# Chunk steps at explicit places, sums in place of clamps, and weight narrowing shared with ScalarE: one change to a fused gated-recurrence and feed-forward kernel

## The chip, the cores and the metric

The kernel runs on one NeuronCore of a Trainium2 chip. The metric is device time in microseconds (us) of one execution. A core has five engines with a queue each: TensorE (PE: matmuls, transposes; its weight loads are listed as PEld), VectorE (DVE), ScalarE (ACT), GpSimd (POOL) and SyncE (SP, which here only issues transfers). The kernel is written in a framework that tracks which instruction needs which tile, gives each tile a place in a pool, and schedules: it fixes the order of each engine's instructions when the program is built. The order in the source is the priority; an instruction whose inputs are ready by the framework's own timing may be put ahead of an earlier one. At run time each engine takes its instructions strictly in the fixed order.

## The reference

Two blocks. The first is a recurrence with complex gates, for 4 batches x 8 heads x 768 steps, head size 48:

```python
mag = np.sqrt(a_re * a_re + a_im * a_im)
scale = np.minimum(mag, 0.999) / (mag + 1e-06)
a_re_n, a_im_n = a_re * scale, a_im * scale
for t in range(S):
    S = a[t] * S + outer(k[t], v[t])        # complex a, per row of S
    y[t] = q[t] @ real(S)
```

The second takes y as 3,072 tokens x 384 and computes, with weights given as float64,

```python
h = x @ w_in                                   # 384 -> 2048
sp = np.maximum(h, 0.0) + np.log1p(np.exp(-np.abs(h)))
out = (h * erf(sp)) @ w_out                    # 2048 -> 384
```

## The kernel before

A unit is 256 tokens of one batch (two chunks of 128); there are 12. Everything of a unit is: its gates; the recurrence of its two chunks; its feed-forward in two slabs of 1,024 hidden columns; the output product.

*Gates.* `g_tan` squares a_re and a_im on ACT, adds on POOL, and makes the tangent: a clamp of a_re from below (L734), a reciprocal (L735), a product with a_im (L740), clamps of |a|^2 (L743) and of the tangent (L745). `g_turn` takes the arctangent on ACT; `g_angle` sums angles over the chunk with a matmul, brings the last row of the chunk before over by a small transfer (L761) and takes whole turns off; `g_sin` makes cosine and sine (tile CS, two buffers). `g_log` makes log magnitudes, `g_decay` sums them with a matmul (L805) and takes exponentials of both signs (tile pr, two buffers). A sum over `off` and `spans` at the end tells whether all values stayed in the range of this path; if not, a branch runs a slower second path (`product_path`).

*Chunk.* `chunk(u, c)` returns eleven steps: k and q times decay and turn (`prep`, L831 and L835), transposes into columns (`cols`, evacuated by ACT, L846), the scores with their mask (`scores`, L854 and L857), the state (`state`, L866 to L875), y (`y_`, evacuated by ACT, L890) and the transpose of y into x^T (`xT`, L899).

*Feed-forward.* `ff_in` makes h of a slab with 48 matmuls, evacuated by ACT (L916). `softplus` clamps h into z on DVE (L930), then runs Exp, Ln, Ln, Exp over 128 x 2,048 elements on ACT, into z and yy. `erf_times_h` works in four parts: t = z * yy on POOL (L948), then DVE and a Gelu on ACT that overwrites z, up to h times erf in place (L949, L951, L952). `ff_out` makes the output in 16 x 2 matmuls (L966), evacuated by ACT (L970). z and yy have one buffer each, h has four.

*Weights.* [...] `narrow` loads a piece as pairs of 32-bit words into a buffer of h and rebuilds float32 with integer operations: five passes on DVE and three more through `words` (a buffer of z), a product (L689) and a sum (L693) on POOL. There are six pieces of w_in (128 x 1,024) and eight of w_out (128 x 768).

*Order.* ACT holds tables for one set of functions at a time; every activation issued through `act` (L639) stands in one fixed chain in source order, with a table load (L638) at each change of set. Plain copies are outside of that chain. The source order comes from windows w = -2 to 13. Window w has the recurrence of unit w, the feed-forward of unit w-1, the output of unit w-2 and the gates of later units; `weave` spreads each list over a share of the window:

```python
wts = weights_in() if w == -1 else weights_out() if w == 0 else []
weave((0.0, 1.0, rec), (0.0, 0.05, only(w + 2, g_turn) + only(w + 1, g_sin)), (0.0, 0.9, wts),
      (0.0, 0.45, f0), (0.45, 0.9, f1), (0.2, 1.0, only(w - 2, ff_out)), ...)
```

Of the kernel before, what the change touches and what calls it, by code (L numbers as in the profile page):

```python
# [19 lines left out]
P = 128  # L20
# [9 lines left out]

SLOPE = 1.5

SPAN = 1e13
# [522 lines left out]
def quotient_path(  # L556
# [49 lines left out]
    dram = ctx.enter_context(tc.tile_pool(name="dram", bufs=4, space=bass.MemoryType.DRAM))  # L606
    ps_a = ctx.enter_context(tc.tile_pool(name="ps_a", bufs=2, space=PSUM))
# [17 lines left out]
    off = const.tile([P, NU], FP, name="off")  # L625
    spans = const.tile([P, NU * C], FP, name="spans")
# [36 lines left out]
    def load_qkv(u):  # L663
        if u < NU:
            load(ldq, "q", q, u)
            load(ldq, "k", k, u)
            load(ldq, "v", v, u, bufs=2)


    def narrow(dst, src, shape):  # L670
# [4 lines left out]
        raw = hp.tile([P, n], I64, tag="h", name="raw")  # L675
        tmps = zp.tile([P, 2, n], U32, tag="z", name="words")
# [5 lines left out]
        a, b = tmps[:, 0], tmps[:, 1]  # L682
        nc.vector.tensor_scalar(out=a, in0=hi, scalar1=0x7FF00000, scalar2=None, op0=OP.bitwise_and)
        nc.vector.tensor_scalar(out=b.bitcast(FP), in0=a, scalar1=float(897 << 20), scalar2=None, op0=OP.is_ge)
# [4 lines left out]
        nc.gpsimd.tensor_tensor(out=f, in0=f, in1=b.bitcast(FP), op=OP.mult)  # L689
        nc.vector.tensor_scalar(out=a, in0=u, scalar1=0xFF800000, scalar2=None, op0=OP.bitwise_and)  # L690
        nc.vector.scalar_tensor_tensor(out=b.bitcast(FP), in0=lo, scalar=2.0**-52, in1=a.bitcast(FP),
                                       op0=OP.mult, op1=OP.mult)
        nc.gpsimd.tensor_tensor(out=f, in0=f, in1=b.bitcast(FP), op=OP.add)  # L693

    def weights_in():
# [3 lines left out]
        return [partial(narrow, w_in_sb[:, i, f0:f0 + n], w_in[i * P:(i + 1) * P, f0:f0 + n], (n,))  # L699
                for f0 in range(0, FF, n) for i in range(KD)]  # L700

    def weights_out():
        if w_out.dtype == FP:
            return [lambda: nc.gpsimd.dma_start(out=w_out_sb, in_=w_out.rearrange("(i p) e -> p i e", p=P))]
        return [partial(narrow, w_out_sb[:, i:i + 2, :].rearrange("p i e -> p (i e)"),
                        w_out[i * P:(i + 2) * P, :].rearrange("(i p) e -> p i e", p=P), (2, DM))
# [11 lines left out]
    def g_tan(u):  # L718
# [3 lines left out]
        def s0():  # L722
            s, y, m = t_("s"), t_("y"), t_("m")
            act(out=s, in_=ar, func=AF.Square)
# [4 lines left out]
            act(out=m, in_=m, func=AF.Relu, accum_out=off[:, u:u + 1])  # L729
            T["s"], T["y"] = s, y  # L730

        def s1():
            rec = t_("rec")
            nc.vector.tensor_scalar(out=rec, in0=ar, scalar1=2.0**-60, scalar2=None, op0=OP.max)  # L734
            nc.vector.reciprocal(out=rec, in_=rec)  # L735
            T["rec"] = rec

# [245 lines left out]
    for f in g_tan(0):  # L983
        f()
# [82 lines left out]
```

## Time and profile before

| what | value |
|---|---|
| time, median of 3 runs | 985.98 us (983.36 to 987.53) |
| the profiled execution's own time | 981.68 us |
| its span, first to last instruction | 980.0 us |
| PE, DVE, ACT, POOL busy | 812.8, 632.6, 579.6, 309.4 us |
| granted clock of PE, mean | 0.922 |
| x^T of a unit complete: units 0, 1, 2, 10, 11 | 128, 177, 313.5, 841.3, 901.3 us |

A row of a group reads: line, engine, operation, tiles out<-in, shapes, count, then busy time (us), mean duration of one (ns), and the idle time of the engine just before these instructions with what ended it. Matmuls overlap, so their mean is longer than their spacing. In the timeline a row starts with start and duration in us. The granted clock is the share of full speed that PE was given.

### The profile page before, as it was taken

How to read it: one execution, taken by the hardware profiler on the slowest of the kernel's cores; microseconds unless marked ns; L12 is line 12 of the kernel's file. 1: busy time of each engine (PE TensorE's matmuls, PEld its weight loads, DVE VectorE, ACT ScalarE, POOL GpSimd, SP SyncE). 2: the span in 40 equal slices, each digit the busy share in tenths (PEclk: the TensorE clock that was granted, in tenths of full speed). 3: DMA queues.
4: the chain of work that ended last, by engine and by line, in shares of the span. 5: the costliest groups of instructions: out<-in, count | busy, mean ns of one | idle time of the engine just before them, and what ended most of it. 6: DMA issues, size and time to landing. Idle time of an engine off the chain costs nothing. (4 is left out here: it accounts for less than half of the span.)

```text
span 980.0 us, 10235 instructions
## 1 busy us (share of the span) xinstructions
PE 812.8 (83%) x3882; PEld 618.2 (63%) x3882; DVE 632.6 (65%) x736; ACT 579.6 (59%) x737; POOL 309.4 (32%) x180
## 2 busy tenths in 40 slices
PE   0115788968849989999999898998999999999987
PEld 0004677755637767777767676776767786887654
DVE  6778987638687576865975965767647534664340
ACT  4515241236777777758568587677684766556650
POOL 3565443324342242431431423224302220132220
PEclk9998575888978989999999999999999899999989
DMA  7552333101030211120311211111011110000000
GB/s 171 133 151 71 86 81 97 49 0 33 2 77 19 34 33 33 33 49 18 65 33 23 43 33 34 33 33 33 7 27 34 33 33 1 17 1 17 1 16 20
DMA packets 148034, 41.77 MB, mean 43 GB/s; under 512 B 142068, under 2 KB 145160, under 8 KB 147208
## 3 DMA queue, kind: packets, MB, share of 16 engines
q1 hardware_dynamic: 147976, 41.03, 18.4%
q8 instruction: 32, 0.52, 0.2%
q14 instruction: 26, 0.21, 0.1%
HBM read 36.24 MB, written 4.75 MB: 42 GB/s over the span
## 5 line engine op out<-in xcount | busy, mean ns | idle before, releaser
L966 PE MATMUL ops<-w_out_sb,h 128*128 128x384 f32 x768 | 286.0, 512 | 16.6 <-DVE h L952 8.9
L914 PE MATMUL hps<-xT,w_in_sb 128*128 128x256 f32 x1152 | 267.8, 387 | 16.9 <-ACT h L916 14.6
L914 PEld LDWEIGHTS hps<-xT,w_in_sb 128*128 128x128 f32 x1152 | 220.3, 194 | 59.0 <-ACT h L916 15.9
L948 POOL TENSOR_TENSOR t<-z,yy 128x512 f32<-128x512 f32 x96 | 148.0, 1560 | 301.0 <-ACT yy L639 261.3
L639 ACT ACTIVATE z<-z 128x2048 f32<-128x2048 f32 (+1 forms) x144 | 152.2, 1057 | 119.9 <-POOL t L948 84.8
L966 PEld LDWEIGHTS ops<-w_out_sb,h 128*128 128x128 f32 x768 | 146.3, 200 | 99.7 <-issue 16.9
L949 DVE SCALAR_TENSOR_TENSOR yy<-t,yy 128x512 f32<-128x512 f32 x96 | 101.6, 1083 | 74.0 <-POOL t L948 74.0
L916 ACT COPY h<-hps 128x512 f32<-128x512 f32 x96 | 55.5, 581 | 86.1 <-PE hps L914 85.4
L951 DVE TENSOR_TENSOR z<-z,yy 128x512 f32<-128x512 f32 x96 | 88.0, 946 | 0.0
L882 PE MATMUL y<-v,A 128*128 128x48 f32 x384 | 77.2, 298 | 11.5 <-DVE A L857 11.5
L857 DVE TENSOR_TENSOR A<-sc,triu 128x512 f32<-128x512 f32 x48 | 32.7, 684 | 79.4 <-PE sc L854 79.4
L638 ACT ACT_TABLE_LOAD x64 | 82.1, 1283 | 1.1
L854 PEld LDWEIGHTS sc<-qT,kT 96*128 96x128 f32 x384 | 54.6, 214 | 44.5 <-ACT qT L846 40.3
L930 DVE TENSOR_SCALAR z<-h 128x1024 f32<-128x1024 f32 x48 | 42.2, 887 | 62.1 <-ACT h L916 59.9
L854 PE MATMUL sc<-qT,kT 96*128 96x128 f32 x384 | 61.0, 308 | 24.4 <-ACT qT L846 23.8
L765 PE MATMUL sum<-th,turns 128*128 128x384 f32 x48 | 26.4, 637 | 65.7 <-DVE th L762 50.6
L952 DVE SCALAR_TENSOR_TENSOR h<-z,h 128x512 f32<-128x512 f32 x96 | 78.4, 846 | 0.1
L882 PEld LDWEIGHTS y<-v,A 128*128 128x128 f32 x384 | 65.1, 216 | 16.1 <-DVE A L857 12.9
L885 PE MATMUL y<-S,qT 96*128 96x48 f32 x320 | 69.3, 302 | 0.0
L793 POOL TENSOR_TENSOR lr<-s,y 128x768 f32<-128x768 f32 x12 | 24.9, 2078 | 127.1 <-ACT y L639 97.0
L735 DVE RECIPROCAL rec<-rec 128x768 f32<-128x768 f32 x12 | 59.4, 4950 | 0.3
L885 PEld LDWEIGHTS y<-S,qT 96*128 96x128 f32 x320 | 56.0, 218 | 0.0
(80 smaller groups left out, 972.4 us busy)
## 6 DMA issues: line engine op xcount, KB each, us to landing
raw<-in_moe_w_in_dram SPq DMA_DIRECT2D x6, 1024.0 KB, 7.1
raw<-in_moe_w_out_dram SPq DMA_DIRECT2D x8, 768.0 KB
ar<-in_a_re_dram SPq DMA_DIRECT2D x24, 192.0 KB, 3.2
ai<-in_a_im_dram SPq DMA_DIRECT2D x24, 192.0 KB, 3.4
q<-in_q_dram SPq DMA_DIRECT2D x24, 192.0 KB, 3.6
k<-in_k_dram SPq DMA_DIRECT2D x24, 192.0 KB, 2.9
v<-in_v_dram SPq DMA_DIRECT2D x24, 192.0 KB, 3.8
out_dram<-o SPq DMA_DIRECT2D x24, 192.0 KB, 1.9
```

Source lines behind the costliest of these rows:

```text
L638: in_order(nc.scalar.preload_act_table_set(sets[0]))
L639: in_order(nc.scalar.activation(func=func, **kw))
L735: nc.vector.reciprocal(out=rec, in_=rec)
L854: nc.tensor.matmul(out=ps[:, j, :], lhsT=st["k", g][0:D2, j, :], rhs=st["q", g][0:D2, j, :], start=True, stop=True)
L882: nc.tensor.matmul(out=y[:, j, :], lhsT=st["A", g][:, i, :], rhs=T["v", u][:, c, j, :], start=True, stop=first)
L885: nc.tensor.matmul(out=y[:, j, :], lhsT=st["q", g][0:D2, i, :], rhs=T["S"][0:D2, j, :], start=False, stop=True)
L914: nc.tensor.matmul(out=ps[:, e, :], lhsT=w_in_sb[:, kd, f0:f0 + P], rhs=T["xT", u][:, kd, :], start=(kd == 0), stop=(kd == KD - 1))
L948: nc.gpsimd.tensor_tensor(out=t, in0=z, in1=y, op=OP.mult)
L949: nc.vector.scalar_tensor_tensor(out=y, in0=t, scalar=-2.0, in1=y, op0=OP.add, op1=OP.mult)
L951: nc.vector.tensor_tensor(out=z, in0=z, in1=y, op=OP.mult)
L952: nc.vector.scalar_tensor_tensor(out=h, in0=z, scalar=1.0 / RT2, in1=h, op0=OP.add, op1=OP.mult)
L966: nc.tensor.matmul(out=ps, lhsT=T["h", u, sl][:, e, jj * P:(jj + 1) * P], rhs=w_out_sb[:, i, :], start=(i == 0), stop=(i == KF - 1))
```

## The change

Six things change together.

1. `weave` gives way to explicit places. Each step of window w gets a number from 0 to 1 and the steps are issued in that order. A chunk's steps have places of their own, with the state and all transposes ahead of the scores. Weights are narrowed in windows -1 (two pieces), 0 (six) and 1 (six).
2. `narrow` has its own pool for the raw words (two buffers) and puts `words` into z and yy by turns. Two DVE passes and POOL's product go; Square and Exp on ACT with a sum take their place (they flag a zero weight), and the low words are scaled on ACT.
3. The clamps go: of h ahead of Exp, of a_re, |a|^2 and the tangent. Sums of squares, of exponentials and of reciprocals, taken by the activations that make these values (`accum_out`), are compared with limits at the end. The reciprocal of a_re becomes Ln and Exp on ACT.
4. In `erf_times_h` the product t moves from POOL to DVE, and Gelu writes a tile e (two buffers) in place of z.
5. The evacuations of q^T, of y and of the output move from ACT to DVE.
6. CS and pr have one buffer; the sums of `g_decay` become steps of their own; sine and arctangent come at the end of a window.

```diff
+    seen = [const.tile([P, n], FP, name=f"seen{i}") for i, n in enumerate((NU * C, NU, NU, NU * NSL, NU * NSL, 16))]
+    spans, off, large, exps, inverse, zeros = seen
     def narrow(dst, src, shape, i):
-        raw = hp.tile([P, n], I64, tag="h", name="raw")
-        tmps = zp.tile([P, 2, n], U32, tag="z", name="words")
+        raw = rawp.tile([P, n], I64, tag="raw", name="raw")
+        pool, tag = ((zp, "z"), (yp, "yy"))[i % 2]
+        tmps = pool.tile([P, 2, n], U32, tag=tag, name="words")
-        nc.vector.tensor_scalar(out=a, in0=hi, scalar1=0x7FF00000, scalar2=None, op0=OP.bitwise_and)
-        nc.vector.tensor_scalar(out=b.bitcast(FP), in0=a, scalar1=float(897 << 20), scalar2=None, op0=OP.is_ge)
+        act(out=b, in_=hi.bitcast(FP), func=AF.Square)
+        act(out=b, in_=b, func=AF.Exp, scale=-1e10, accum_out=zeros[:, i:i + 1])
...
-        nc.gpsimd.tensor_tensor(out=f, in0=f, in1=b.bitcast(FP), op=OP.mult)
+        nc.scalar.mul(out=b, in_=lo, mul=2.0**-52)
...
-        nc.vector.scalar_tensor_tensor(out=b.bitcast(FP), in0=lo, scalar=2.0**-52, in1=a.bitcast(FP),
-                                       op0=OP.mult, op1=OP.mult)
+        nc.vector.tensor_tensor(out=b, in0=b, in1=a.bitcast(FP), op=OP.mult)
...
     def g_log(u):
+            act(out=m, in_=ar, func=AF.Ln)
+            act(out=m, in_=m, func=AF.Exp, scale=-1.0)
...
+            nc.gpsimd.tensor_tensor(out=th.rearrange("p c f -> p (c f)"), in0=m, in1=ai, op=OP.mult)
...
     def cols(nm, g):
-                nc.scalar.copy(out=t[0:D2], in_=ps[0:D2])
+                (nc.scalar.copy if nm == "k" else nc.vector.tensor_copy)(out=t[0:D2], in_=ps[0:D2])
...
-        return [prep("k", 1), prep("q", 0), cols("k", 0), cols("k", 1), cols("q", 0), scores(0), cols("q", 1),
-                scores(1), state, y_, xT]
+        return [(0.0, prep("k", 1)), (0.03, prep("q", 0)), (0.06, cols("k", 0)), (0.09, cols("k", 1)),
+                (0.12, cols("q", 0)), (0.15, cols("q", 1)), (0.2, state), (0.25, scores(0)), (0.28, scores(1)),
+                (0.36, y_), (0.45, xT)]
...
     def softplus(u, sl):
-            for i in range(0, SLAB, half):
-                nc.vector.tensor_scalar(out=z[:, i:i + half], in0=h[:, i:i + half], scalar1=8.0, scalar2=-16.0,
-                                        op0=OP.min, op1=OP.max)
-            act(out=z, in_=z, func=AF.Exp)
+            act(out=z, in_=T["h", u, sl], func=AF.Exp, accum_out=exps[:, i:i + 1])
...
     def erf_times_h(u, sl):
-                nc.gpsimd.tensor_tensor(out=t, in0=z, in1=y, op=OP.mult)
+                act(out=e, in_=z, func=AF.Gelu, scale=RT2)
+                nc.vector.tensor_tensor(out=t, in0=z, in1=y, op=OP.mult)
...
     for w in range(-2, NU + 2):
+        plan = [(0.62, partial(load_qkv, w + 1)), (0.72, partial(load_gates, w + 3))]
+        if 0 <= w < NU:
+            plan += [(0.5 * c + p, f) for c in range(C) for p, f in chunk(w, c)]
+        if w == -1:
+            plan += at(0.0, 0.8, weights_in()[:2])
+        elif w == 0:
+            plan += at(0.0, 0.7, weights_in()[2:]) + at(0.75, 1.0, weights_out()[:2])
+        elif w == 1:
+            plan += at(0.0, 0.3, weights_out()[2:])
+        plan += at(0.0, 1.0, only(w - 2, ff_out))
+        if 0 <= w - 1 < NU:
+            for sl in range(NSL):
+                b = 0.06 + 0.4 * sl
+                plan += at(b, b + 0.24, ff_in(w - 1, sl))
+                plan += [(b + 0.25, softplus(w - 1, sl))]
+                plan += at(b + 0.3, b + 0.42, erf_times_h(w - 1, sl))
+        plan += at(0.05, 0.1, only(w + 2, g_mag))
+        plan += at(0.1, 0.45, only(w + 1, g_angle))
+        plan += at(0.68, 0.71, only(w + 1, g_decay))
+        plan += at(0.712, 0.714, only(w + 2, g_log))
+        plan += at(0.9, 0.95, only(w + 1, g_sin) + only(w + 2, g_turn))
+        for _, f in sorted(plan, key=lambda e: e[0]):
+            f()
```

`at(begin, end, steps)` spreads steps evenly over a share of the window. `g_mag` is what is left of `g_tan`: the squares, their sum and the range test.

123 lines of the change are left out of this document (49 added, 74 removed).

## The prediction

> **What bounds the kernel now.** I read the page first: which engine is busy, and when.
>
> ```profile
> span 980.0 us, 10235 instructions
> PE 812.8 (83%) x3882; PEld 618.2 (63%) x3882; DVE 632.6 (65%) x736; ACT 579.6 (59%) x737; POOL 309.4 (32%) x180
> PE   0115788968849989999999898998999999999987
> PEclk9998575888978989999999999999999899999989
> ```
>
> One digit is 24.5 us. From the thirteenth slice on TensorE (PE) is nearly full; before that it isn't, and its clock is often granted at half. So the kernel has two bounds, and I cut the span into stages. Columns: the stretch, its length, busy time with instruction count of PE, weight loads, DVE, ACT, POOL, then clock and DMA.
>
> ```profile
> 31.60:211.80 180.20, 118.69 (x510) 95.88 (x510) 141.91 (x158) 56.90 (x94) 81.95 (x38) 0.79 0.32 85
> 313.50:841.30 527.80, 494.81 (x2549) 379.88 (x2548) 343.57 (x411) 369.32 (x472) 151.95 (x88) 0.98 0.16 31
> 841.30:901.30 60.00, 59.80 (x314) 46.15 (x312) 32.66 (x45) 36.01 (x44) 12.74 (x8) 1.00 0.02 8
> 901.30:980.00 78.70, 65.95 (x223) 44.06 (x222) 25.44 (x37) 30.85 (x33) 10.71 (x8) 0.91 0.04 14
> 375.30:444.90 69.60, 65.49 (x338) 50.03 (x336) 48.08 (x55) 47.59 (x62) 21.00 (x12) 0.98 0.17 35
> 375.30:713.00 337.70, 315.02 (x1624) 239.63 (x1622) 233.76 (x270) 237.65 (x306) 103.99 (x59) 0.99 0.17 33
> ```
>
> The cuts are the landings of the second half of x^T of a unit (row 313.5 is unit 2's, 841.3 unit 10's, 901.3 unit 11's). Eight units in 527.8 us are 66.0 each; PE is busy 494.81, or 61.9 each. The ninth, without gate work, takes 60.0 with no PE idle. The steady part is PE's, with 4 us a unit to win.
>
> The first stage ends where the last weight is narrowed. The tile "words" shows it (min/median/max ns, first and last start), and so does ACT's timeline:
>
> ```profile
> L683 DVE TENSOR_SCALAR words<-raw x14: 497/561/2280, 31.6 to 203.6; 128x768 uint32<-128x768 uint32 x8, 128x1024 uint32<-128x1024 uint32 x6
> L691 DVE SCALAR_TENSOR_TENSOR words<-raw,words x14: 940/958/1225, 39.2 to 208.8; 128x768 f32<-128x768 uint32 x8, 128x1024 f32<-128x1024 uint32 x6
> L687 DVE SCALAR_TENSOR_TENSOR w_in_sb<-raw,words x6: 1205/1218/2817, 34.1 to 115.8; 128x1024 uint32<-128x1024 uint32 x6
> L689 POOL TENSOR_TENSOR w_in_sb<-w_in_sb,words x6: 2332/2348/3943, 35.4 to 117.1; 128x1024 f32<-128x1024 f32 x6
> L693 POOL TENSOR_TENSOR w_out_sb<-w_out_sb,words x8: 1798/1808/1993, 133.8 to 210.0; 128x768 f32<-128x768 f32 x8
> 213.17 3.85 ACT L639 ACTIVATE z<-z 128x2048 f32<-128x2048 f32 x2 [8.32 <-DVE z L930]
> ```
>
> Fourteen narrowings run one behind the other from 31.6 to 211.8 us (210.0 plus 1.8): 12.9 us each, because all share the one buffer of z. The first softplus needs that buffer too and starts at 213.17. So the feed-forward of unit 0 waits for the last weight. That is the first bound.
>
> **The change, part by part.** The rows that price it:
>
> ```profile
> L948 POOL TENSOR_TENSOR t<-z,yy 128x512 f32<-128x512 f32 x96 | 148.0, 1560 | 301.0 <-ACT yy L639 261.3 <-DVE Skv L874 24.6 <-DVE yy L949 15.1
> L949 DVE SCALAR_TENSOR_TENSOR yy<-t,yy 128x512 f32<-128x512 f32 x96 | 101.6, 1083 | 74.0 <-POOL t L948 74.0
> L951 DVE TENSOR_TENSOR z<-z,yy 128x512 f32<-128x512 f32 x96 | 88.0, 946 | 0.0
> L952 DVE SCALAR_TENSOR_TENSOR h<-z,h 128x512 f32<-128x512 f32 x96 | 78.4, 846 | 0.1
> L949 DVE SCALAR_TENSOR_TENSOR yy<-t,yy x96: 672/678/2305, 223.0 to 954.7; 128x512 f32<-128x512 f32 x96
> L735 DVE RECIPROCAL rec<-rec 128x768 f32<-128x768 f32 x12 | 59.4, 4950 | 0.3
> L930 DVE TENSOR_SCALAR z<-h 128x1024 f32<-128x1024 f32 x48 | 42.2, 887 | 62.1 <-ACT h L916 59.9 <-POOL w_out_sb L693 2.0
> L743 DVE TENSOR_SCALAR s<-s 128x768 f32<-128x768 f32 x12 | 13.7, 1139 | 8.2 <-POOL s L726 8.2
> L745 DVE TENSOR_SCALAR th<-rec 128x768 f32<-128x768 f32 x12 | 11.8, 984 | 0.0
> L734 DVE TENSOR_SCALAR rec<-ar 128x768 f32<-128x768 f32 x12 | 6.7, 554 | 7.5 <-DMA ar<-in_a_re_dram 6.3 <-issue 1.2
> L835 DVE TENSOR_TENSOR kt<-kr,CS x24: 940/945/2723, 77.3 to 864.9; 128x768 f32<-128x768 f32 x24
> L846 ACT COPY qT<-tr 96x512 f32<-96x512 f32 x48 | 27.6, 574 | 13.0 <-PE tr L843 13.0
> L890 ACT COPY x<-y 128x384 f32<-128x384 f32 x24 | 11.1, 464 | 31.3 <-PE y L885 29.9 <-PE y L882 1.4
> L970 ACT ACTIVATE o<-ops 128x384 f32<-128x384 f32 x24 | 11.5, 483 | 25.1 <-PE ops L966 22.8 <-PEq L1035 2.1
> L639 ACT ACTIVATE s<-s 128x768 f32<-128x768 f32 x12 | 10.2, 847 | 0.0
> L639 ACT ACTIVATION_READ_ACCUMULATOR pr<-sum 128x1 f32 x24 | 5.0, 207 | 0.0
> ```
>
> *Load per unit.* DVE loses the reciprocal (4.95), four clamps of h (4 x 0.887 = 3.5) and three of the gates (0.55 + 1.14 + 0.98): 11.1 us. It gains eight products t, for which no DVE row exists: the like L949 takes 0.672 at least and 2.305 at most, and I take the median, 0.68, so 5.4 us. It gains eight evacuations (four q^T, two x, two o): below by the 0.46 that ACT takes, above by the 0.95 of kt, the longest undisturbed DVE operation of a chunk; I take 0.55, 4.4 us. And the three multiplications behind t, with means of 1.08, 0.95 and 0.85 against 0.68, lose the excess that stands beside POOL's t: 8 x 0.84 = 6.7 us. DVE goes from 46.8 (233.76 / 5) to about 39. POOL loses 8 x 1.56 = 12.5. ACT loses 4 x 0.574 + 2 x 0.464 + 2 x 0.483 = 4.2 us and gains two gate activations (1.7) and five accumulator reads (1.0): 47.5 (237.65 / 5) becomes 46. PE's work stays. None of these totals reaches 60, so their worth lies in PE's waits:
>
> ```profile
> PE xt L898 <- ACT x L890: 8.8, 6, 2.7
> PE sc L854 <- ACT qT L846: 7.1, 8, 1.7
> ACT z L639 <- POOL t L948: 38.1, 37, 1.7
> ```
>
> These are the waits of five steady units, 375.3 to 713 (total us, times, longest). PE waited 15.9 us, 3.2 a unit, for the q^T and x copies that queue on ACT behind activations of up to 1.9 us; on DVE nothing undisturbed is longer than about 0.95. ACT's 7.6 us a unit for POOL go, as Gelu now writes a tile of its own. Against that stands just-in-time order: CS and pr have one buffer, and sine and cosine of the next unit stand after the last Gelu of the window, so a new chunk waits for ACT's queue. A Gelu block goes at the pace of DVE's 16 operations, 9.6 us at 0.6 each (the 0.68 less what neighbours overlap, an estimate), of which ACT works 2.5: two blocks add some 14 us of waiting to 46 busy, and ACT comes near 60 itself. The product DVE now makes queues ahead of the chunk's own DVE work, which PE waits for. So I take half of what is there: 64.0 a unit instead of 66.0, eight units, 16 us; the bounds are 61.9 (PE never idle, 33 us won) and 70 (ACT leads, 32 lost).
>
> *Startup.* A narrowing loses two DVE passes and POOL's product and gains Square, Exp and a copy on ACT. It alternates between z and yy for words and has two raw buffers of its own. Per w_in piece: ACT 3 x 1.06 + 0.2 (1.06 from 0.847 at 768 columns and 1.92 at 2048, below), DVE about 0.7 + 1.2 + 0.7 + 1.2, POOL 2.3.
>
> ```profile
> 219.67 1.92 ACT L639 ACTIVATE yy<-yy 128x2048 f32<-128x2048 f32 x1
> raw<-in_moe_w_in_dram SPq DMA_DIRECT2D x6, 1024.0 KB, 7.1
> q<-in_q_dram SPq DMA_DIRECT2D x24, 192.0 KB, 3.6
> L638 ACT ACT_TABLE_LOAD x64 | 82.1, 1283 | 1.1
> ```
>
> The chain of one piece is some 9 us, the load before it 7.1, and two can be under way: (7 + 5) / 2 = 6 us each. Fourteen make 84. They begin about where they do now, near 30, since unit 0's gates come first. Every activation goes in one fixed order, so narrowings stand between the gate steps of units 1 and 2 and lose about 11 us to them. First softplus at 30 + 84 + 11 = 125, against 213: 88 us. The loads of gates, q, k and v move to 0.62 and 0.72 of a window, on SP behind the raw loads; they land in about 3.6 us and are first used a quarter of a unit (16 us) later, which hides them; uncovered they cost those 3.6 a unit. The steps of a chunk, of the decay and of the angle are the same instructions in other places, on queues with idle time. Bounds of the first softplus: 105 (ACT's 3.4 plus table loads alone, under 5 us a piece) and 175 (10 us a piece, with every wait behind gate steps). From first softplus to 313.5 the chain stays at 100 us; what the shorter erf saves I give to the later CS.
>
> The narrowings between trigonometric steps cost two or three extra table loads, 1.3 us each by the row above, inside the 11. The Trainium skill (ScalarE: Activation LUTs, What ACT_TABLE_LOAD costs) puts a switch at 2.66 us with a drain, which would make that up to 8 us; the load rows here leave no such gap. The same page (Rules for kernel authors) would keep multiplications on VectorE, against the copy with 2^-52 that moves to ACT; no run here prices that copy.
>
> *End.* The last erf block gets shorter, and with it the wait ahead of the last 64 matmuls:
>
> ```profile
> 951.05 23.40 PE L966 MATMUL ops<-w_out_sb,h 128*128 128x384 f32 x64 [4.65 <-ACT o L970]
> ```
>
> I take 5 us, the 4.65 and a little; bounds 0 and 12.7 (78.70 less 65.95 busy). The four extra sums at the very end are hidden under these matmuls; uncovered they would cost about 1.
>
> **Sum.** 980.0 - 88 - 16 - 5 = 871 span. The profiled execution took 981.68, so 1.7 lies around its span; the median of the timed runs, 985.98, is 4.3 above it. 871 + 1.7 + 4.3 = 877.
>
> **Rivals.** (a) ACT's order becomes the steady bound, 69.6 us a unit as the fullest unit now (375.3 to 444.9): 8 x 5.6 = 45 more than the forecast, 922. For it: 46 of 64 us busy in strict order. Against: half of each window's waits of ACT go.
> (b) The narrowings stay slow behind gate activations, 10 us each: first softplus at 175, 927. For it: the one activation order. Against: DVE has two passes fewer and two buffers run.
> (c) PE stays full: 61.9 a unit and softplus at 105: 877 - 17 - 20 = 840.
> (d) Slower: DVE's queue. The eight evacuations stand behind an erf block part (4 x 0.6 = 2.4 us) and PE has nothing else to do: 8 x 8 x 2.4 = 154 us over eight units in place of the 16 won: 877 + 16 + 154 = 1,047. It makes the kernel slower from (986 - 893) / 64 = 1.45 us exposed at each evacuation. Against: PE has feed-forward matmuls in between.
> (e) The change doesn't do what it says: one of the range sums exceeds its limit, and the branch runs the other path: at least another 12 x 60 us of matmuls, over 1,600. From the inputs h lies within 0.11 of zero, and all six sums are well below their limits; only a table that misbehaves at huge negative arguments would do it.
>
> **How the numbers follow.** Forecast 0.37, (a) 0.22, (b) 0.12, (c) 0.19, (d) 0.06, (e) 0.02, and 0.02 for no change by accidents that cancel. Faster by over 0.5%, about what a measurement can tell here, is the first four: 0.90; within 0.5% 0.02; slower 0.08. The range takes in (a) to (c) with a little beyond their ends: 835 to 940.
>
> **What would show it.** The first Exp of softplus near 125 (105 to 175), words alternating between two tiles at about 6 us; units at 64 us with PE waits for q^T and x gone; L948's product on DVE at 0.68. Wrong: a first softplus past 175, or ACT without idle time while PE waits for kt at the start of each unit.

## The result

The changed kernel takes 870.4 us (median of 4 runs, 868.99 to 878.88), the kernel before 984.7 us (977.97 to 987.53) on the same chip. The ratio is 0.886, with a 95% interval of 0.880 to 0.893. The profiled execution was the longest of the four, 878.88 us with a span of 876.7; a second profile of the same kernel on another chip (the control below) has a span of 868.5.

The page of the changed kernel: busy time and count of PE, then 40 slices of 21.9 us each with PE's busy tenths and its granted clock.

```profile
span 876.7 us, 10225 instructions
PE 774.6 (88%) x3882; PEld 603.3 (69%) x3882; DVE 550.2 (63%) x813; ACT 602.1 (69%) x783; POOL 124.6 (14%) x70
PE   0166983989989999999989999999899999999996
PEclk9765787879999999999999999999999999999999
```

TensorE is nearly full (8 or 9) from the eighth slice, 153 us, on; before it was from the thirteenth, 294 us. POOL's busy time fell from 309 to 125 us. The same cuts as in the prediction (columns: stretch, length, busy time of PE, weight loads, DVE, ACT, POOL, clock, DMA):

```profile
27.30:145.70 118.40, 80.21 (x383) 64.73 (x382) 98.27 (x107) 86.71 (x128) 48.00 (x22) 0.72 0.46 122
145.70:230.40 84.70, 73.69 (x370) 58.49 (x371) 52.76 (x81) 64.46 (x82) 7.53 (x5) 0.85 0.17 31
230.40:748.40 518.00, 498.35 (x2593) 390.69 (x2592) 322.55 (x500) 367.20 (x477) 56.74 (x30) 0.98 0.17 35
748.40:806.70 58.30, 58.23 (x311) 46.15 (x310) 35.22 (x56) 36.52 (x43) 0.00 (x0) 1.00 0.02 8
806.70:876.70 70.00, 62.05 (x226) 42.27 (x224) 30.79 (x58) 31.68 (x35) 0.00 (x0) 0.98 0.05 16
```

x^T of unit 2 is complete at 230.4 instead of 313.5, of unit 10 at 748.4 instead of 841.3, of unit 11 at 806.7 instead of 901.3. So of the 103.3 us by which the two profiled spans differ, 83.1 lie ahead of unit 2, 9.8 in the eight steady units (518.0 against 527.8), 1.7 in unit 11 and 8.7 behind it (70.0 against 78.7). The change is above all a change of the startup. In the eight steady units PE's idle time fell by more than the length, from 33.0 to 19.7 us, as PE's busy time grew from 494.8 to 498.4: 44 more of the matmuls stand there, and 44 fewer ahead of unit 2. How the startup looks, by the tile of the narrowing (min/median/max ns, first and last start) and by one row of ACT's timeline:

```profile
L692 DVE TENSOR_SCALAR words<-raw x14: 541/616/2839, 10.1 to 137.8; 128x768 uint32<-128x768 uint32 x8, 128x1024 uint32<-128x1024 uint32 x6
L644 ACT ACTIVATE words<-raw x14: 881/942/1167, 27.3 to 135.1; 128x768 f32<-128x768 f32 x8, 128x1024 f32<-128x1024 f32 x6
L696 ACT ACTIVATE words<-raw x14: 869/930/1150, 31.7 to 142.0; 128x768 f32<-128x768 uint32 x8, 128x1024 f32<-128x1024 uint32 x6
L699 POOL TENSOR_TENSOR w_out_sb<-w_out_sb,words x8: 1807/2066/2530, 93.9 to 143.9; 128x768 f32<-128x768 f32 x8
```

```profile
140.06 1.91 ACT L644 ACTIVATE z<-h 128x2048 f32<-128x2048 f32 x1 [3.11 <-POOL w_out_sb L699]
```

From the first Square at 27.3 to the end of the last sum at 145.7 a narrowing takes 118.4 / 14 = 8.5 us, where it took 12.9. (The first DVE pass starts at 10.1, by the first row; counted from there it is 9.7.) The first softplus starts at 140.1, 73 us earlier; it still waits for a weight (POOL's L699).

The wait that is left in the steady part, in five units from 295.3 to 619.1 (total us, times, longest), and one instance of it in the timeline:

```profile
ACT e L644 <- DVE h L947: 26.1, 15, 4.4
...
PE tr L843 <- DVE kt L835: 11.1, 5, 3.3
```

```profile
364.38 2.10 POOL L789 TENSOR_TENSOR lr<-s,y 128x768 f32<-128x768 f32 x1 [3.61 <-DVE s L788]
364.84 2.19 DVE L944 TENSOR_TENSOR t<-z,yy 128x512 f32<-128x512 f32 x1
...
369.59 1.23 ACT L644 ACTIVATE e<-z 128x512 f32<-128x512 f32 x2 [3.10 <-DVE h L947]
370.73 0.83 ACT L644 ACTIVATE m<-F 128x768 f32<-128x768 f32 x1
371.58 1.28 ACT L643 ACT_TABLE_LOAD   x1
372.87 0.93 ACT L644 ACTIVATE CS<-m,half_pi 128x768 f32<-128x768 f32 x1
373.71 0.83 ACT L644 ACTIVATE CS<-F 128x768 f32<-128x768 f32 x1
...
374.57 0.96 DVE L835 TENSOR_TENSOR kt<-kr,CS 128x768 f32<-128x768 f32 x1 [1.82 <-ACT CS L644]
...
375.59 1.08 PE L843 MATMUL tr<-ident,kt 128*96 128x128 f32 x8 [1.96 <-DVE kt L835]
```

Read it from the bottom: PE waits 1.96 us for kt, kt for sine and cosine, these stand in ACT's one order behind the last Gelu of the window, and that Gelu waited 3.1 us for DVE's erf products, one of which took 2.19 us instead of 0.68 beside POOL's subtraction. The evacuations of q^T and x no longer make PE wait.

### The profile page after: what moved, and what is told of

It is laid out like the page before. It is cut to its first block, busy times and chain, and to the rows that moved or that the text cites. A ratio compares the mean times of both kernels' runs of the same rounds, so it can differ in the third digit from the quotient of the medians.

```text
span 876.7 us, 10225 instructions
## 1 busy us (share of the span) xinstructions
PE 774.6 (88%) x3882; PEld 603.3 (69%) x3882; DVE 550.2 (63%) x813; ACT 602.1 (69%) x783; POOL 124.6 (14%) x70
## 4 chain that ended last, share of the span: by engine, by line
PE 66%; DVE 17%; ACT 8%; issue 6%; POOL 2%; DMA 0%; SPq 0%; POOLq 0%; DVEq 0%; ACTq 0%
PE ops L961 23%; PE hps L915 17%; PE tr L843 5%; PE y L882 5%; PE sc L854 4%; PE y L885 4%; DVE t L944 4%; DVE yy L945 3%; PE kv L866 3%; PE sum L756 2%; DVE kt L835 2%; DVE e L946 2%; ACT m L644 1%; ACT e L644 1%; PE sum L817 1%
## 5 line engine op out<-in xcount | busy, mean ns | idle before, releaser
L961 PE MATMUL ops<-w_out_sb,h 128*128 128x384 f32 x768 | 272.2, 500 | 13.7 <-DVE h L947 13.7
L944 DVE TENSOR_TENSOR t<-z,yy 128x512 f32<-128x512 f32 x96 | 82.4, 858 | 32.6 <-ACT yy L644 31.3
L644 ACT ACTIVATE e<-z 128x512 f32<-128x512 f32 x96 | 57.7, 627 | 59.3 <-DVE h L947 59.0
L643 ACT ACT_TABLE_LOAD x66 | 84.7, 1283 | 1.1
L787 POOL TENSOR_TENSOR th<-m,ai 128x768 f32<-128x768 f32 x12 | 22.6, 1884 | 372.7 <-ACT m L644 372.7
L882 PE MATMUL y<-v,A 128*128 128x48 f32 x384 | 71.3, 280 | 3.5 <-DVE A L857 3.5
L945 DVE SCALAR_TENSOR_TENSOR yy<-t,yy 128x512 f32<-128x512 f32 x96 | 68.8, 717 | 1.2
L843 PE MATMUL tr<-ident,kt 128*96 128x128 f32 x192 | 31.8, 309 | 40.7 <-DVE kt L835 40.7
L946 DVE TENSOR_TENSOR e<-e,yy 128x512 f32<-128x512 f32 x96 | 64.7, 687 | 4.6 <-DVE yy L945 0.5
L947 DVE SCALAR_TENSOR_TENSOR h<-e,h 128x512 f32<-128x512 f32 x96 | 64.5, 685 | 0.7
L843 PEld LDWEIGHTS tr<-ident,kt 128*96 128x96 f32 x192 | 24.5, 142 | 52.0 <-DVE kt L835 46.9
L890 DVE COPY x<-y 128x384 f32<-128x384 f32 x24 | 13.4, 557 | 74.6 <-PE y L885 65.0
```

What stands on the lines that cost most here:

```text
L643: in_order(nc.scalar.preload_act_table_set(sets[0]))
L644: in_order(nc.scalar.activation(func=func, **kw))
L843: nc.tensor.transpose(out=ps[0:D2, j, :], in_=st[nm][:, g * HG + j].rearrange("p u d -> p (u d)"), identity=ident)
L882: nc.tensor.matmul(out=y[:, j, :], lhsT=st["A", g][:, i, :], rhs=T["v", u][:, c, j, :], start=True, stop=first)
L944: nc.vector.tensor_tensor(out=t, in0=z, in1=y, op=OP.mult)
L945: nc.vector.scalar_tensor_tensor(out=y, in0=t, scalar=-2.0, in1=y, op0=OP.add, op1=OP.mult)
```

## The experiments

All kernels below are compared in one table; "xT2" is the time of x^T of unit 2, here and above the start of its last copy, which takes 0.48 us; "eight units" is the time from there to unit 10. The PE idle time in these eight units is the length less PE's busy time in that stretch, and the clock is PE's granted clock there.

| kernel | median us | ratio to before, 95% | first softplus | xT2 | eight units | of it PE idle | clock | per unit | behind unit 11 |
|---|---|---|---|---|---|---|---|---|---|
| before (profile) | 984.7 | 1 | 213.2 | 313.5 | 527.8 | 33.0 | 0.98 | 65.97 | 78.7 |
| changed (profile) | 870.4 | 0.886, 0.880 to 0.893 | 140.1 | 230.4 | 518.0 | 19.7 | 0.98 | 64.75 | 70.0 |
| control: changed, again | 870.2 | 0.883, 0.877 to 0.889 | 139.6 | 225.0 | 514.9 | 19.7 | 0.98 | 64.36 | 70.2 |
| words in z alone | 887.5 | 0.896, 0.889 to 0.903 | 154.7 | 238.2 | 516.1 | 19.7 | 0.98 | 64.51 | 71.3 |
| old arithmetic | 901.8 | 0.915, 0.909 to 0.922 | 167.5 | 253.8 | 516.1 | 19.7 | 0.98 | 64.51 | 70.0 |
| clamps, reciprocal back | 892.7 | 0.907, 0.903 to 0.912 | 153.7 | 249.4 | 517.1 | 22.0 | 0.99 | 64.64 | 69.9 |
| before + two buffers | 985.8 | 0.995, 0.991 to 1.000 | 191.1 | 304.5 | 540.5 | 31.6 | 0.97 | 67.56 | 78.2 |
| before + places | 984.2 | 0.997, 0.994 to 1.001 | 196.2 | 295.4 | 552.3 | 33.3 | 0.95 | 69.04 | 71.2 |
| evacuations back on ACT | 857.4 | 0.865, 0.858 to 0.871 | 132.3 | 221.5 | 509.2 | 12.4 | 0.98 | 63.65 | 69.3 |
| sine early | 842.0 | 0.849, 0.843 to 0.856 | 136.6 | 222.9 | 493.3 | 3.8 | 1.00 | 61.66 | 70.0 |
| t on POOL | 903.6 | 0.919, 0.911 to 0.928 | 141.1 | 233.3 | 537.9 | 28.0 | 0.95 | 67.24 | 69.9 |
| Gelu in z | 887.7 | 0.902, 0.895 to 0.908 | 140.7 | 229.6 | 529.3 | 21.8 | 0.96 | 66.16 | 70.0 |
| evacuations + sine | 833.3 | 0.849, 0.844 to 0.854 | 130.4 | 217.7 | 492.3 | 0.0 | 0.99 | 61.54 | 69.2 |
| the same, words in h | 830.2 | 0.845, 0.840 to 0.849 | 112.0 | 215.7 | 490.2 | 0.8 | 1.00 | 61.27 | 69.0 |

### The changed kernel again, as a control

> The changed kernel itself, as a control beside the next three on one chip. Both theories: the ratio to the kernel before as measured, 0.886 (0.880 to 0.893).

870.2 us (869.47 to 870.6) and a span of 868.5. It is 8.2 us shorter than the first profile of the same program: 5.4 ahead of unit 2 and 3.1 in the eight units, with the same eight pauses of PE. Two more spells of half clock in the first profile account for about the 3.1 us (see the last section). Differences of 5 us in xT2 and of 0.4 us a unit between two profiles are therefore not read as effects below. Experiments on the changed kernel are compared with the control.

### The startup: one buffer, the arithmetic, the clamps

Words in z alone, as before:

```diff
-        pool, tag = ((zp, "z"), (yp, "yy"))[i % 2]
+        pool, tag = (zp, "z")
```

> The changed kernel with words in z alone again; arithmetic, raw buffers and places as changed. Theory 1 (sharing one buffer for words made the narrowings a chain, and with it the startup): a piece holds z from its first DVE pass to POOL's sum, some 9 us, so the first softplus moves from 140 to about 160 to 170 and the time from 870 to 890 to 900. Theory 2 (one chain of activations and the places set the pace, not the buffer): first softplus within 5 us of 140, time within 6 us of 870.

887.5 us: 17 us above the control, xT2 13 us later. So the shared buffer, which the prediction named as the first bound, is worth 13 to 17 us of the 114.

The same alternation, put alone into the kernel before:

```diff
-        tmps = zp.tile([P, 2, n], U32, tag="z", name="words")
+        pool, tag = ((zp, "z"), (yp, "yy"))[i % 2]
+        tmps = pool.tile([P, 2, n], U32, tag=tag, name="words")
```

> The kernel before with one part alone: words go to z and yy by turns. Theory 1: pieces overlap and the first softplus comes from 213 to 180 or earlier; VectorE was busy 142 of the 180 us of that stage, so at most about 38 us can be won; time 950 to 965. Theory 2: the places and VectorE's own queue hold the pieces; under 10 us won, 975 or more.

985.8 us, ratio 0.995: next to nothing. The last narrowing ended at 182.3 instead of 211.7, but x^T of unit 1 came at 238.6 instead of 176.9. The stretch 31.6 to 211.8 of this kernel:

```profile
31.60:211.80 180.20, 79.80 (x347) 62.68 (x348) 158.22 (x155) 62.91 (x93) 97.24 (x43) 0.99 0.31 83
```

DVE is busy 158.2 of 180.2 us (88%), where it was busy 141.9 (79%) before, and PE only 79.8 instead of 118.7: the narrowings moved ahead of the recurrence's own work in DVE's queue. A buffer was what one narrowing waited for; behind it stood an engine with hardly any time left. x^T of unit 2 still came 9 us earlier, but the eight units behind it took 12.7 us more, with 35 more matmuls in them, so part of what the startup won was work put off.

The old arithmetic in the changed kernel's buffers and places. It flags a zero weight by its own exponent test and not by the sum of Square and Exp, so that sum is left out:

```diff
-        act(out=b, in_=hi.bitcast(FP), func=AF.Square)
-        act(out=b, in_=b, func=AF.Exp, scale=-1e10, accum_out=zeros[:, i:i + 1])
+        nc.vector.tensor_scalar(out=a, in0=hi, scalar1=0x7FF00000, scalar2=None, op0=OP.bitwise_and)
+        nc.vector.tensor_scalar(out=b, in0=a, scalar1=float(897 << 20), scalar2=None, op0=OP.is_ge)
...
-        nc.scalar.mul(out=b, in_=lo, mul=2.0**-52)
+        nc.gpsimd.tensor_tensor(out=f, in0=f, in1=b, op=OP.mult)
...
-        nc.vector.tensor_tensor(out=b, in0=b, in1=a.bitcast(FP), op=OP.mult)
+        nc.vector.scalar_tensor_tensor(out=b, in0=lo, scalar=2.0**-52, in1=a.bitcast(FP), op0=OP.mult, op1=OP.mult)
```

> The changed kernel with the narrowing arithmetic of before (five passes on VectorE and two on GpSimd, nothing on ScalarE) in the new buffers and places. Theory 3 (less work and fewer mutual blocks on VectorE and GpSimd are what shortened the startup, since the buffer alone won nothing and undoing it lost 1%): x^T of unit 2 comes 30 to 50 us later than 230 and the time grows by 30 to 50 us, ratio 0.92 to 0.94. Theory 4 (the places did it): under 15 us, ratio below 0.90.

901.8 us, 32 above the control; first softplus 28 us later, xT2 29 us later, the eight units as they were.

The clamps and the reciprocal back on DVE, with Ln and Exp of a_re gone:

```diff
-            act(out=m, in_=ar, func=AF.Ln)
-            act(out=m, in_=m, func=AF.Exp, scale=-1.0)
+            nc.vector.tensor_scalar(out=m, in0=ar, scalar1=2.0**-60, scalar2=None, op0=OP.max)
+            nc.vector.reciprocal(out=m, in_=m)
+            nc.vector.tensor_scalar(out=s, in0=s, scalar1=2.0**-63, scalar2=2.0**63, op0=OP.max, op1=OP.min)
...
+            nc.vector.tensor_scalar(out=th.rearrange("p c f -> p (c f)"), in0=th.rearrange("p c f -> p (c f)"),
+                                    scalar1=SLOPE, scalar2=-SLOPE, op0=OP.min, op1=OP.max)
...
-            act(out=z, in_=T["h", u, sl], func=AF.Exp, accum_out=exps[:, i:i + 1])
+            for a in range(0, SLAB, SLAB // 2):
+                nc.vector.tensor_scalar(out=z[:, a:a + SLAB // 2], in0=T["h", u, sl][:, a:a + SLAB // 2], scalar1=8.0,
+                                        scalar2=-16.0, op0=OP.min, op1=OP.max)
+            act(out=z, in_=z, func=AF.Exp, accum_out=exps[:, i:i + 1])
```

> The changed kernel with the clamps of h and of the gates and the reciprocal on VectorE again (Ln and Exp of a_re go); the range sums stay. Theory 5 (VectorE's queue stands in front of Gelu, sine and kt, so 11 us a unit more of it are paid in part): 2 to 3 us more a unit and 5 to 10 at the start, ratio 0.90 to 0.92. Rival (VectorE is idle 40% of a unit and takes it for nothing): within 6 us of the changed kernel, ratio 0.88 to 0.89.

892.7 us, 23 above the control, all of it in the startup: xT2 24 us later, a unit 0.3 us longer, which is within what two profiles of one kernel differ by. The first 160 us of this kernel, DVE's groups by line:

```profile
L782 DVE RECIPROCAL m<-m 128x768 f32<-128x768 f32 x4 | 19.8, 4942 | 0.0
...
L783 DVE TENSOR_SCALAR s<-s 128x768 f32<-128x768 f32 x4 | 8.6, 2141 | 12.7 <-POOL s L732 12.7
...
L789 DVE TENSOR_SCALAR th<-th 128x768 f32<-128x768 f32 x4 | 5.9, 1483 | 1.2 <-POOL th L788 1.2
```

Four units' gates are made in these 160 us, the first of them before 27.3, and the operations of these three rows are 34 us of DVE; in the steady part the same operations come once in 65 us and cost nothing that can be told.

DVE's share of the stretch from the first Square (27.3) to the first softplus, in the control, with the old arithmetic, with the clamps, and with words in z alone:

```profile
27.30:139.60 112.30, 79.46 (x382) 64.58 (x380) 94.14 (x102) 80.89 (x122) 46.17 (x21) 0.80 0.48 128
```

```profile
27.30:167.50 140.20, 87.33 (x383) 71.00 (x383) 116.18 (x129) 42.64 (x68) 74.28 (x35) 0.69 0.39 105
```

```profile
27.30:153.70 126.40, 80.05 (x349) 65.05 (x349) 112.43 (x113) 79.92 (x120) 55.97 (x25) 0.67 0.43 115
```

```profile
27.30:154.70 127.40, 77.78 (x382) 63.80 (x380) 87.11 (x110) 83.21 (x124) 44.60 (x22) 0.81 0.43 113
```

84%, 83%, 89% and 68%. Put 22 us of work back on DVE (116.2 against 94.1) and the first softplus comes 28 us later; put 18 back and it comes 14 later. Take a buffer away and DVE stands idle instead. The old arithmetic also puts a product back on POOL (74.3 us of POOL against 46.2), so the busy times alone don't tell DVE from POOL. The chain of work that ended last does: followed through these four stretches and added up by engine, DVE's part is 43 us in the control and 72 with the old arithmetic, POOL's 9 and 8. With the clamps DVE's part is 51 and POOL's 21, with words in z alone 24 and 21. With two buffers DVE is thus the largest part of the startup's chain (43 of 112 us, ahead of 31 of PE and 17 of ACT), though not all of it; with one buffer it no longer is.

### The places alone

The kernel before, with the changed kernel's plan and order of a chunk's steps, its own arithmetic, clamps, engines and buffers (the last step of the tangent at 0.5):

```diff
-        weave(
...
+        plan = [(0.62, partial(load_qkv, w + 1)), (0.72, partial(load_gates, w + 3))]
...
+        for _, f in sorted(plan, key=lambda e: e[0]):
+            f()
```

> The kernel before with one part alone: the explicit places of the change (chunk steps, narrowings, gates, sine), old arithmetic, buffers, clamps and engines; the last gate step, which writes the tangent, stands at 0.5 of a window, since its one buffer is read until 0.45. Theory 3: words in one buffer and the old arithmetic still hold the startup, x^T of unit 2 at 280 us or later, time 960 or more. Theory 4: x^T of unit 2 comes before 260, and the time falls to 920 to 940.

984.2 us, ratio 0.997: no gain. But inside it three terms cancel: xT2 at 295.4, 18 us earlier; 69.04 us a unit, 3.1 more, which makes 25 in eight units; 71.2 us behind unit 11, 7.5 less. The places alone are thus worth 26 us at both ends and cost the same between. PE's idle time in the eight units is as before, 33 us. What grew is the time at half clock, from 24 to 55 us, which is 15 of the 25, and 61 more matmuls stand in the stretch:

```profile
295.40:847.70 552.30, 518.98 (x2610) 402.34 (x2610) 359.05 (x437) 380.16 (x491) 161.64 (x95) 0.95 0.16 32
```

In the startup this kernel has a hole, PE busy 8.25 of 50 us:

```profile
150.00:200.00 50.00, 8.25 (x24) 6.46 (x24) 23.94 (x35) 6.05 (x6) 19.80 (x11) 0.59 0.15 47
```

The waits of this stretch say why:

```profile
ACT h L917 <- DVE words L691: 32.8, 1, 32.8
...
PE hps L915 <- ACT h L917: 28.4, 1, 28.4
```

ACT's copy of h waits 32.8 us for L691, the pass that reads a raw weight for the last time, since raw words still live in buffers of h here; PE's feed-forward matmuls wait behind that copy. So the raw buffers of their own, which the prediction named and put no price on, are probably what lets the places work in the startup; no run has these places with such buffers and the rest as before, so this is argued from the wait and not shown.

### The steady part: evacuations, sine, the product t, Gelu's tile

The evacuations of q^T, x and the output back on ACT:

```diff
-                (nc.scalar.copy if nm == "k" else nc.vector.tensor_copy)(out=t[0:D2], in_=ps[0:D2])
+                nc.scalar.copy(out=t[0:D2], in_=ps[0:D2])
...
-            nc.vector.tensor_copy(out=x, in_=y.rearrange("p h d -> p (h d)"))
+            nc.scalar.copy(out=x, in_=y.rearrange("p h d -> p (h d)"))
...
-                    nc.vector.tensor_scalar(out=o, in0=ps, scalar1=-RT2, scalar2=None, op0=OP.mult)
+                    nc.scalar.mul(out=o, in_=ps, mul=-RT2)
```

> The changed kernel with q^T, y and the output evacuated by ScalarE again. Theory 1 (these copies on ScalarE cost PE 3.2 us a unit before): PE waits for q^T and x come back and the time grows by 15 to 30 us, to 885 to 900. Rival (the scheduler places them where ScalarE is free, and the gain per unit comes from other parts): within 5 us of 870.

857.4 us (855.67 to 858.01): 13 us faster than the changed kernel. This part of the change costs time. Waits of this kernel from 295 to 600 us:

```profile
ACT e L644 <- DVE h L947: 6.8, 7, 3.3
```

The control has 26.1 us of that wait in the same stretch. PE does wait for q^T again, 3.2 us in that stretch, but its wait for kt fell from 11.1 to 2.8 us. With the copies gone from DVE's queue the erf products end earlier, so Gelu, so sine, so kt.

Sine and arctangent at 0.72 of the window, ahead of the second erf block, and not at 0.9 behind it:

```diff
-        plan += at(0.9, 0.95, only(w + 1, g_sin) + only(w + 2, g_turn))
+        plan += at(0.72, 0.74, only(w + 1, g_sin) + only(w + 2, g_turn))
```

> The changed kernel with sine, cosine and arctangent at 0.72 to 0.74 of a window, ahead of the last Gelu block instead of behind it; same number of table loads. Theory 1 (the one PE wait left per unit, for kt behind sine and cosine, is what keeps units at 64.75 us against 62.3 busy): that wait of 2.2 to 3.7 us a unit goes, and the time falls by 15 to 25 us, to 845 to 855. Rival (the later Gelu block takes it back: h of the second slab comes 5 us later and the output matmuls wait): within 5 us of 870 or slower.

842.0 us (840.71 to 844.02): 28 faster than the control, and 61.66 us a unit. The eight units of this kernel and of the control:

```profile
222.90:716.20 493.30, 489.52 (x2601) 386.88 (x2600) 325.03 (x504) 371.24 (x481) 61.50 (x30) 1.00 0.19 37
```

```profile
225.00:739.90 514.90, 495.19 (x2593) 388.94 (x2592) 322.45 (x500) 367.03 (x476) 56.75 (x30) 0.98 0.18 35
```

PE's wait for kt from 230 to 716 us, in the first profile of the changed kernel and in this one:

```profile
PE tr L843 <- DVE kt L835: 19.6, 8, 3.3
```

```profile
PE tr L843 <- DVE kt L835: 3.8, 3, 1.3
```

PE's idle time in the eight units goes from 19.7 to 3.8 us. The wait for kt is the last thing that keeps PE from being full, and one moved line takes it away.

The product t back on POOL, Gelu still with its own tile:

```diff
-                nc.vector.tensor_tensor(out=t, in0=z, in1=y, op=OP.mult)
+                nc.gpsimd.tensor_tensor(out=t, in0=z, in1=y, op=OP.mult)
```

> The changed kernel with t = z * yy on GpSimd again; Gelu still writes its own tile. Theory 1 (GpSimd's product and its blocks on VectorE stood in the erf chain, and so in front of Gelu, sine and kt): 1.5 to 4 us more a unit, 15 to 40 us in all, ratio 0.90 to 0.93. Rival (VectorE is relieved of 5.4 us a unit, which its queue needs as much): within 6 us of the changed kernel.

903.6 us, 67.24 us a unit, 2.9 more than the control. The end is as short as with t on DVE (69.9). The eight units of this kernel, and below them those of the next one, Gelu in z:

```profile
233.30:771.20 537.90, 509.85 (x2593) 397.90 (x2592) 314.16 (x436) 366.86 (x476) 142.76 (x95) 0.95 0.17 34
229.60:758.90 529.30, 507.49 (x2593) 398.33 (x2592) 331.16 (x500) 366.32 (x476) 60.52 (x30) 0.96 0.17 34
```

Of the 23.0 us by which t on POOL is longer than the control there, 8.3 are idle time of PE. The rest is the same number of matmuls at a lower clock: PE is at half clock for 51 us, where the control has 17, and half of the difference is 17 us.

Gelu back in z, t still on DVE:

```diff
-                act(out=e, in_=z, func=AF.Gelu, scale=RT2)
...
+                act(out=z, in_=z, func=AF.Gelu, scale=RT2)
-                nc.vector.tensor_tensor(out=e, in0=e, in1=y, op=OP.mult)
-                nc.vector.scalar_tensor_tensor(out=h, in0=e, scalar=1.0 / RT2, in1=h, op0=OP.add, op1=OP.mult)
+                nc.vector.tensor_tensor(out=z, in0=z, in1=y, op=OP.mult)
+                nc.vector.scalar_tensor_tensor(out=h, in0=z, scalar=1.0 / RT2, in1=h, op0=OP.add, op1=OP.mult)
```

> The changed kernel with Gelu writing into z in place again, so that the tile e of its own is gone; the product t stays on VectorE. Theory (with t on VectorE the wait of Gelu for t is short, and the gain of 2.9 us a unit that the run with t on GpSimd showed belongs to the engine alone): within 6 us of 870, units of 64 to 65. Rival (the tile of its own carries part of that gain: Gelu now queues behind VectorE's products, and sine, kt and the next unit's transposes queue behind Gelu): 1 to 2 us more a unit, 880 to 890.

887.7 us, 17 above the control, and 66.16 us a unit: the rival's time held. From 290 to 620 us ACT waits for DVE's products ahead of Gelu:

```profile
ACT z L644 <- DVE t L942: 20.7, 15, 1.9
```

The control has 26.1 us of such waits in the same stretch, ahead of its tile e, so this wait isn't longer than there. The rival's path isn't seen either: PE's wait for kt from 230 to 716 us is 11.7 us, where the control has 19.7. By the second row above, of the 14.4 us by which the eight units are longer 2.1 are idle time of PE, and the rest is the same number of matmuls at a lower clock: 44 us at half clock against 17.

So by time the two halves of this edit belong together. With t on POOL or with Gelu in z a unit takes 67.2 or 66.2 us, no better than before; only with both does it take 64.4. Most of that difference goes through PE's clock; why Gelu in z keeps the clock at half for longer stays open.

### What they add up to

Not undone by themselves were the raw buffers, the single buffers of CS and pr, and the loads of gates, q, k and v at later places. Two kernels were run with the findings put together. The first has the evacuations back on ACT and the early sine:

> The changed kernel with both edits that won: evacuations of q^T, y and output on ScalarE, and sine, cosine and arctangent ahead of the last Gelu block. If they act on different waits: 13 us below the early sine alone, ratio 0.835 to 0.84. If the evacuations only shortened the same wait for kt: as the early sine alone, ratio 0.845 to 0.855.

833.3 us (832.33 to 838.02), and in the eight units PE is busy without a gap:

```profile
217.70:710.00 492.30, 492.30 (x2612) 389.56 (x2611) 308.13 (x445) 393.67 (x545) 62.78 (x30) 0.99 0.18 37
```

By the ratio, 0.849 both times, it isn't told apart from the early sine alone, which ran on another chip; the medians differ by 9 us, and a unit takes the same (61.54 and 61.66). That fits with the harm of the evacuations going through the wait for kt: without that wait little of it is left in a unit.

The second also puts the words of the narrowing into buffers of h, so that softplus shares no buffer with them, and spreads the last six pieces over window 1:

```diff
-        pool, tag = ((zp, "z"), (yp, "yy"))[i % 2]
-        tmps = pool.tile([P, 2, n], U32, tag=tag, name="words")
+        tmps = hp.tile([P, 2, n], U32, tag="h", name="words")
...
-            plan += at(0.0, 0.3, weights_out()[2:])
+            plan += at(0.0, 0.9, weights_out()[2:])
```

> Both edits that won, and words in buffers of h (two of its four are free then) with the last six narrowings spread to 0.9 of window 1. Theory 6 (what holds the first softplus now is that z and yy hold words until the last narrowing): first softplus at 115 to 125 instead of about 135, x^T of unit 2 before 212, 8 to 15 us won on top. Rival (the order of activations holds it, whatever the buffer): under 4 us.

830.2 us (827.59 to 832.9), the fastest kernel here, 0.845 of before. The first softplus starts at 112.0, 18 us earlier than in the kernel it was made from, but x^T of unit 2 only 2 us earlier. What sets the startup behind the first softplus of that kernel was not found.

## Why the prediction was right, and where its steps were wrong

The time came out 7 us below the forecast, and the sign and the place (startup first, then a little of everything) were right. It is closer than its terms are: the first softplus came 15 us late and the chain behind it was 10 us shorter, and in the steady part a move of the wrong sign and terms at no price cancel. That closeness is in part luck. Step by step:

*The first bound, the z buffer.* The chain on that buffer was really there, but only a small part of the gain came from it. Undone one at a time in the changed kernel, xT2 comes later by 13 us (buffers), 29 (arithmetic), 24 (clamps and reciprocal) and 8 (t and POOL), and earlier by 3.5 (evacuations); the places alone brought 18 in the kernel before. The sum, 89, happens to be what the control won there (313.5 to 225.0, 88.5); such terms need not add up. The prediction quoted DVE at 141.91 of 180.20 us in this stage and then sized the new one by a buffer's turn and a load's time.

*First softplus at 125, narrowings at 6 us with 11 for gates.* Measured 140.1, and 8.5 us each with the gate steps between. The step that was mis-sized is (7 + 5) / 2 = 6 us: it lacked DVE's queue, where a narrowing's passes stand between the work of three units. No row gives its 5; with the "some 9 us" that the prediction names for the chain of a piece it would be (7 + 9) / 2 = 8, near the 7.7 that remain when the 11 us for gates are taken off the 118.4.

*"From first softplus to 313.5 the chain stays at 100 us."* It became 90.3 (85.4 in the control): this missed term covers most of what the first softplus came late. It is no constant: putting the clamps back makes it 95.7, putting t back on POOL 92.2, words in z alone 83.5 and words in h 103.7. In that stretch DVE was busy 69.6 of 98.5 us before, by the trace, and is now 52.8 of 84.7.

*Clamps and reciprocal.* Counted as 11.1 us of DVE a unit, spread evenly. In the steady part they are worth nothing that can be told; in the startup 24 us, where four units' gates crowd into 160 us. The load per unit was right and its average hid the stage.

*Steady part, 64.0.* Measured 64.75 and 64.36, the sum nearly right out of parts that were not. (1) Moving the evacuations was to take away 3.2 us of PE's waits a unit; the waits went, but the kernel is 13 us faster without the move: wrong in sign. (2) Moving t and giving Gelu its own tile was to free ACT of 7.6 us of waiting a unit. Taking back one of the two does cost 2.9 or 1.8 us a unit, so the sign was right; but ACT now waits 5.2 us a unit for DVE instead (26.1 in five units), and most of what the two runs lose is PE's clock, for which the prediction has no term. (3) The places were costed at nothing; alone they cost 3.1 us a unit, 1.9 of them by the clock. (4) kt behind sine was named as what stands against the gain, without a price of its own; it is 2.7 us a unit (64.36 to 61.66). The reason, an order of ACT behind the last Gelu, was the right one.

*The end, 5 us, by a shorter erf block.* It was 8.7, but the cause failed: the places alone win 7.5 of it with the old erf block, and with t on POOL the end stays at 69.9.

*Table loads.* 66 instead of 64, at 1,283 ns:

```profile
L643 ACT ACT_TABLE_LOAD x66 | 84.7, 1283 | 1.1
...
L846 DVE COPY qT<-tr 96x512 f32<-96x512 f32 x48 | 31.9, 682 | 15.5 <-PE tr L843 15.4
```

In the timeline above the load ends at 372.86 and the next activation starts at 372.87. The Trainium skill (ScalarE: Activation LUTs, What ACT_TABLE_LOAD costs) gives the same 1,283 ns and adds a drain of 1,380; no such gap shows here behind the load.

*The rivals.* (a) ACT's order as the bound, at 69.6 us a unit: not reached, though ACT's order is what the wait for kt consists of. (b) Narrowings at 10 us, softplus at 175: no, though both measured values (8.5 us, 140) lie between the forecast's and these. (c) PE full, 61.9 us a unit: not in the changed kernel; with the evacuations back and sine early it is, at 61.5. (d) PE waiting at each evacuation on DVE: no, PE's transposes of x waited 0.7 us in the whole run for it. The evacuations did harm from the other side: they delay the erf products, not PE. (e) The range sums: the fast path was taken.

*What would show it.* The tiles alternate, the waits for q^T and x are gone, t's median on DVE is 0.685 us as taken; its mean is 0.858, since 11 of the 96 take 2.2 us beside POOL. "ACT without idle time while PE waits for kt" isn't what is seen: ACT is idle for 3.1 us ahead of 369.6, waiting for DVE. The chain runs through both engines.

## What to carry to other kernels

A stage that waits on a buffer may have a nearly full engine right behind it: read the busy share of each engine in that stage before pricing the buffer, since freeing the buffer alone (0.995) bought nothing here, and in the changed kernel giving the engine its old work back cost 23 and 32 us. A large gain can hide parts that cost time; undoing each part by itself found 13 us in one and, in the place of one line, 28 us. With engines that keep a strict order, place work that the next unit waits for ahead of long blocks, not by how busy its engine is on average. And look at the granted clock of a stretch beside PE's idle time: three of these experiments lost more by the clock than by waiting.

## What the runs showed of the hardware

*PE's clock halves for 3.4 us behind some pauses, and at places without a pause.* In its eight steady units the changed kernel's PE has eight pauses of 1.95 to 3.29 us, one at the start of each unit. The 8 us behind six of them:

```profile
247.90:255.90 8.00, 8.00 (x52) 6.90 (x53) 4.80 (x8) 5.79 (x11) 3.58 (x2) 0.79 0.01 2
310.20:318.20 8.00, 8.00 (x49) 6.69 (x50) 4.78 (x9) 6.09 (x11) 3.58 (x2) 0.79 0.00 0
375.60:383.60 8.00, 8.00 (x57) 7.07 (x58) 5.24 (x9) 6.09 (x11) 3.60 (x2) 1.00 0.01 2
442.20:450.20 8.00, 7.97 (x51) 6.86 (x52) 4.86 (x8) 5.76 (x11) 3.58 (x2) 0.79 0.00 0
504.60:512.60 8.00, 8.00 (x49) 6.61 (x50) 4.77 (x9) 6.06 (x11) 3.58 (x2) 0.79 0.01 2
570.00:578.00 8.00, 8.00 (x57) 7.07 (x58) 5.23 (x9) 6.07 (x11) 3.59 (x2) 1.00 0.00 0
```

A clock of 0.79 over 8 us is about 3.4 us at half speed, 1.7 us lost. It follows four of the eight pauses in this profile and two in the control's, with pauses of the same length.

Three more such falls in each of these two profiles stand where PE doesn't pause. Each comes right behind 3.4 us filled almost whole with the matmuls of y, which are 48 columns wide. The kernel with the evacuations back and the early sine, whose PE has no gap in the eight units, has two falls, both of this kind. The 3.4 us ahead of one and the 3.4 us of the fall:

```profile
452.50:455.90 3.40, 3.40 (x34) 3.40 (x32) 0.04 (x1) 3.40 (x5) 0.00 (x0) 1.00 0.01 2
455.90:459.30 3.40, 3.40 (x8) 1.89 (x8) 3.30 (x4) 2.50 (x4) 1.55 (x1) 0.50 0.64 153
```

That the clock falls without a pause is shown; that the narrow matmuls bring it about was not tested, and most blocks of y are not followed by a fall. So the first profile of the changed kernel has seven falls in its eight units and the control five, and two falls at 1.7 us are about the 3.1 us between them. In the kernel with the early sine three pauses of 1.26 us and one fall are left; of its 21.6 us against the control, 15.9 are idle time, and the other 5.7 go with the four falls fewer (6.8 us by the same estimate). The Trainium skill (TensorE: Matmul & The Clock Gate, What's actually happening) has the gate fall to half after at least one idle window of about 3.4 us that runs by itself. The half and the 3.4 us agree with these rows; but here pauses of 1.96 us were enough, some of the time, and some falls had no pause ahead of them.

*A product on DVE waits for a running operation of POOL.* In the timeline above t takes 2.19 us and ends 0.55 us behind POOL's subtraction, where t's median is 0.685. All 11 of the 96 products t that take about 2.2 us look like this: each starts while a POOL operation runs and ends 0.55 us behind it. The Trainium skill (SBUF — State Buffer, SBUF: two separate sides) tells of an exclusive lock for a DVE operation with two inputs in SBUF beside a GpSimd operation that reads it; these rows fit. The one shown stands right in the chain to kt.

*An evacuation is longer on DVE.* The copy of q^T, 96 x 512, takes 682 ns there by the row above, against ACT's 574 in the kernel before (by the row in the prediction).
